# The start of the second MLP's tile pool in SBUF, 64 bytes later

## The chip, the cores and the metric

The kernel runs on one core of one Trainium2 chip. A core has five engines that run side by side and meet at semaphores: TensorE (PE in the profile; its weight loads are listed apart as PEld), VectorE (DVE), ScalarE (ACT), GpSimd (POOL) and SyncE (SP, which here issues transfers alone). Operands lie in SBUF, a memory of 128 partitions; TensorE's sums go to PSUM and are read from there by VectorE and ScalarE. A matmul has a stationary operand (the weights, 128 x 128 here, loaded first) and a moving one (here mostly 128 x 512), whose columns stream past the weights. The metric is the device time of one execution in microseconds (us).

## What is computed

Three parts follow on each other, on an input of 4 sequences of 3072 tokens with 256 features, in float32:

```python
X = np.fft.fft(np.fft.fft(x, axis=1), axis=2).real        # [4, 3072, 256]
h = X.reshape(-1, 256) @ w_in                              # first MLP, d_ff 2048
y = np.maximum(0.01 * h, h) @ w_out
x_prev = concat([0, y[:, :-1]], axis=1)                    # second MLP, on y by sequence
xk, xr = mu_k * y + (1 - mu_k) * x_prev, mu_r * y + (1 - mu_r) * x_prev
k = np.maximum(xk @ w_k, 0)                                # w_k 256 x 1024
v = (k * k) @ w_v                                          # w_v 1024 x 256
out = sigmoid(xr @ w_r) * v                                # w_r 256 x 256
```

## The kernel before

Every large product is made of three TensorE products in the type fp32r: each operand is split into a high part (a rounded copy, made by ScalarE) and a low part (what is left, made by VectorE, line L111), and high x high, low x high and high x low are summed in PSUM. Names ending in `h` and `l` are these parts.

The program is written out in full, in a fixed order. The Fourier transform along the sequence (`f..` sums, L299) is woven between the rounds of the first MLP. A round of the first MLP multiplies one 512-token tile by 128 columns of the hidden layer: three matmuls `ps<-Q` (L560), three `ps<-P` (L548) and twelve `o` matmuls (L571, from the round two before), 18 in all, each with a moving operand of 512 columns. Its result `y` goes to DRAM. Near the end of the first MLP two groups of six matmuls of the second one are already issued (`ps`, L884).

The second MLP then goes over 24 tiles of 512 tokens. For each tile it runs 8 rounds: six matmuls `kps` (L884: the moving operands `mh`, `ml` are the tile's mixed input, the weights `wkh`, `wkl`), ScalarE's `rl` (L888), VectorE's square `k` (L889), the split into `k2h` and `k2l`, and, two rounds later, six matmuls `v` (L926: moving `k2h`, `k2l`, weights `wvh`, `wvl`). Two rounds of each tile also have six gate matmuls `rps` (L934). The mixed input of the next tile (`mt`, `mx`, `mh`, `ml`; L730, L731) is made during the tile before.

Where the operands lie: tiles are placed one behind another in pools. The pool `p2` holds what the second MLP makes (`sig`, `rl`, `k2`, `k2h`, `k2l`, the loaded tiles `xa` and `xb`, `mt`, `mx`, the split inputs `mh` and `ml`, and the output `o`). It begins where the first MLP's pool `wp` began, at byte 43936 of each partition. The weights of the second MLP are in the pool `w2p`, at byte 192480 and up. All these tiles are whole multiples of 512 bytes long, and every slice of weights that one matmul takes begins a multiple of 512 bytes behind its tile's start, so that each operand has one place modulo 512. The tile that tile 0 of the second MLP takes its `mh` and `ml` from lies in another pool, `stage`. The places that the program gives (start address modulo 512 bytes), for fp32r matmuls:

| matmuls | moving operand | weights | in the kernel before |
|---|---|---|---|
| first MLP: `ps` L548, L560 and `o` L571 | 416 | 416 | 3456 matmuls |
| `dps` L592 (weights of 2 columns) | 416 | 32 or 64 | 32 |
| transform L299, batches 1 to 3 | 352 to 456, in steps of 8 | 480 | 216 |
| second MLP, inputs from `stage`: `ps`, and tile 0's `kps` L884; `v<-er` L926 | 128 | 480 | 54 |
| second MLP, inputs from `p2`: `kps` L884 | 416 | 480 | 1104 |
| second MLP: `v` L926 | 416 | 480 | 1146 |
| second MLP: `rps` L934 | 416 | 480 | 288 |

Of the kernel before, what the change touches and what calls it, by code (L numbers as in the profile page):

```python
# [9 lines left out]
F32 = mybir.dt.float32  # L10
# [7 lines left out]
P = 128  # L18
# [60 lines left out]
def fft_mlp_kernel(ctx, tc, xa, xb, x7, x8, x87, tb, tbs, alt, ce, so, mu, w_in, w_out, w_k, w_v, w_r, out):  # L79
# [832 lines left out]

    ps2 = ctx.enter_context(tc.tile_pool(name="ps2", bufs=1, space=PSUM))
    p2 = w2["p2"] = ctx.enter_context(tc.tile_pool(name="p2", bufs=2))

    NB = D // P

# [166 lines left out]
```

## Time and profile before

| | before |
|---|---|
| median of 3 runs | 1526.74 us (1526.39 to 1526.97) |
| the profiled execution's own time | 1527.49 us |
| its span, first to last instruction | 1525.7 us |
| TensorE busy | 1495.8 us, 98% |
| VectorE, ScalarE busy | 1032.4 us (68%), 890.5 us (58%) |
| mean granted TensorE clock | 0.997 of full speed |

The span is the time between the first and the last instruction that the profile shows; the execution's own time has 1.8 us more around it. [...]

### The profile page before, as it was taken

What the parts mean: (1) busy time and instruction counts of PE and PEld (TensorE: products, weight loads), DVE (VectorE), ACT (ScalarE), POOL (GpSimd) and SP (SyncE); (2) the same over time, 40 slices, a digit from 0 to 9 for tenths busy, and PEclk for the clock granted to TensorE, in tenths of its full rate; (3) what the DMA queues carried; (4) which work ended last, traced back from release to release, by engine and by line L of the source; (5) the groups of instructions that cost most, each with busy time, mean ns of one, the idle gap of its engine ahead of it and who ended that gap; (6) DMA issues with size and microseconds to landing.
All of it is one profiled execution on the core that took longest, in us unless ns stands there. A gap on an engine that the chain in (4) does not pass through costs nothing.

```text
span 1525.7 us, 17754 instructions
## 1 busy us (share of the span) xinstructions
PE 1495.8 (98%) x6506; PEld 1212.2 (79%) x6506; DVE 1032.4 (68%) x1426; ACT 890.5 (58%) x1469; POOL 168.1 (11%) x165
## 2 busy tenths in 40 slices
PE   5899999999999999999999999999999999999998
PEld 2677888888888888888888887888888888888887
DVE  8776667676667666666667666666666666666664
ACT  2565566566566656665666656555555555555553
POOL 4333401033001132010000000000000000000000
PEclk9999999999999999999999999999999999999999
DMA  7435614276113565132320103121111212121200
GB/s 249 139 94 115 115 52 153 75 184 99 31 66 122 183 114 89 38 126 86 107 78 0 55 1 124 56 70 65 61 63 62 69 56 69 56 69 56 70 29 28
DMA packets 97810, 128.71 MB, mean 84 GB/s; under 512 B 29190, under 2 KB 64775, under 8 KB 94650
## 3 DMA queue, kind: packets, MB, share of 16 engines
q1 hardware_dynamic: 74618, 87.29, 17.7%
q0 software_dynamic: 23104, 40.29, 11.6%
q8 instruction: 51, 0.84, 0.2%
q14 instruction: 37, 0.30, 0.1%
HBM read 99.67 MB, written 27.88 MB: 84 GB/s over the span
## 4 chain that ended last, share of the span: by engine, by line
PE 95%; DVE 1%; DMA 1%; ACT 0%; issue 0%; POOL 0%; ACTq 0%; DVEq 0%
PE o L571 34%; PE v L926 17%; PE kps L884 17%; PE ps L560 9%; PE ps L548 9%; PE rps L934 4%; PE wps L383 1%; PE dps L592 0%; DMA pm<-in_xa 0%; DMA xl<-in_xb 0%; PE cps L434 0%; PE f0Qe L299 0%; PE f0Pe L299 0%; PE f0Po L299 0%; PE f1Qe L299 0%; PE f2Qe L299 0%
## 5 line engine op out<-in xcount | busy, mean ns | idle before, releaser
L637 DVE SCALAR_TENSOR_TENSOR g<-ev,ps 128x512 f32<-128x512 f32 x192 | 131.7, 686 | 193.3 <-PE ps L560 193.2
L888 ACT ACTIVATE rl<-kps 128x512 f32<-128x512 f32 x190 | 113.8, 599 | 245.2 <-PE kps L884 241.6
L889 DVE SCALAR_TENSOR_TENSOR k<-kps,rl 128x512 f32<-128x512 f32 x190 | 131.4, 692 | 163.3 <-ACT rl L888 161.0
L619 DVE TENSOR_TENSOR gl<-g,gh 128x1024 fp32r<-128x1024 f32 x192 | 239.9, 1249 | 1.4 <-ACT gh L104 1.4
L104 ACT ACTIVATE gh<-g 128x1024 fp32r<-128x1024 f32 x192 | 202.8, 1056 | 51.2 <-PE o L571 50.2
L571 PE MATMUL o<-gh,uoh 128*128 128x512 f32 x768 | 211.3, 389 | 0.0
L571 PE MATMUL o<-gh,uol 128*128 128x512 f32 x768 | 211.1, 389 | 0.0
L571 PE MATMUL o<-gl,uoh 128*128 128x512 f32 x768 | 211.1, 389 | 0.0
L107 ACT ACTIVATE g<-ps 128x512 f32<-128x512 f32 x192 | 114.9, 598 | 163.0 <-DVE g L637 161.6
L571 PEld LDWEIGHTS o<-gh,uoh 128*128 128x128 f32 x768 | 144.1, 188 | 30.4
L571 PEld LDWEIGHTS o<-gh,uol 128*128 128x128 f32 x768 | 144.2, 188 | 30.0
L571 PEld LDWEIGHTS o<-gl,uoh 128*128 128x128 f32 x768 | 144.1, 188 | 29.9
L553 DVE SCALAR_TENSOR_TENSOR ev<-cb,w,ps 128x512 f32<-128x512 f32 x192 | 143.4, 747 | 2.6 <-PE ps L548 0.8
L111 DVE TENSOR_TENSOR k2l<-k,k2h 128x512 fp32r<-128x512 f32 x190 | 129.4, 681 | 0.6 <-ACT k2h L104 0.6
L926 PE MATMUL v<-k2h,wvh 128*128 128x512 f32 x382 | 124.1, 396 | 0.1
L926 PE MATMUL v<-k2h,wvl 128*128 128x512 f32 x382 | 124.0, 395 | 0.0
L926 PE MATMUL v<-k2l,wvh 128*128 128x512 f32 x382 | 124.0, 395 | 0.0
L884 PE MATMUL kps<-mh,wkh 128*128 128x512 f32 x380 | 119.7, 396 | 1.5 <-ACT mh L104 0.8
L884 PE MATMUL kps<-ml,wkh 128*128 128x512 f32 x380 | 119.6, 396 | 0.1
L107 ACT ACTIVATE g<-g 128x512 f32<-128x512 f32 x192 | 119.6, 623 | 0.0
L884 PE MATMUL kps<-mh,wkl 128*128 128x512 f32 x380 | 119.5, 396 | 0.0
L104 ACT ACTIVATE k2h<-k 128x512 fp32r<-128x512 f32 x190 | 118.3, 623 | 0.0
(392 smaller groups left out, 2280.3 us busy)
## 6 DMA issues: line engine op xcount, KB each, us to landing
y<-yo SPq DMA_DIRECT2D x24, 512.0 KB
xa<-y SPq DMA_DIRECT2D x24, 512.0 KB
out_dram<-o SPq DMA_DIRECT2D x23, 512.0 KB
tab_c<-in_tbs POOLq DMA_DIRECT2D x6, 1158.0 KB, 5.6
tab_d<-in_tbs POOLq DMA_DIRECT2D x6, 1158.0 KB, 5.5
tab_a<-in_tbs POOLq DMA_DIRECT2D x6, 1158.0 KB, 6.5
tab_b<-in_tbs POOLq DMA_DIRECT2D x6, 1158.0 KB, 5.4
xl<-in_xa SPq DMA_DIRECT2D x24, 256.0 KB
```

The costliest lines, as they stand in the source:

```text
L104: A.activation(o, i, ACTF.Copy)
L107: A.activation(o, i, ACTF.Prelu, alpha=0.01)
L111: V.tensor_tensor(lo, src, hi.bitcast(F32), op=ALU.subtract)
L548: T.matmul(x["ps"], l[:, f], r, start=(i == 0), stop=(i == 2))
L553: V.scalar_tensor_tensor(x["ev"], x["cb"], w128[:, u:u + 1], x["ps"], op0=ALU.mult, op1=ALU.add)
L560: T.matmul(x["ps"], l[:, f], r, start=False, stop=(i == 2), skip_group_check=True)
L571: T.matmul(po[s][h], w[:, u % HF, h * P:(h + 1) * P], g[:, s], start=(u == 0 and i == 0), stop=(u == NF - 1 and i == 2))
L619: V.tensor_tensor(gl, x["g"], x["gh"].bitcast(F32), op=ALU.subtract)
L637: V.scalar_tensor_tensor(g[:, 1], x["ev"], 2.0, x["ps"], op0=ALU.mult, op1=ALU.subtract)
L884: T.matmul(ps, w[:, k, sl], x[:, k], start=(i == 0), stop=(i == 5))
L889: V.scalar_tensor_tensor(k2, ps, 0.0, r, op0=ALU.max, op1=ALU.mult)
L926: T.matmul(vps[m], w[:, f, m * P:(m + 1) * P], x, start=(f == 0 and i == 0), stop=(f == NK - 1 and i == 2))
```

## The change

One line takes a tile of 16 float32 (64 bytes in each partition) at the start of the pool `p2`. No instruction reads or writes it. Everything else in `p2` begins 64 bytes later (`sig` at byte 44000 where it was 43936, and so on), so that `mh`, `ml`, `k2h` and `k2l` of `p2` are at 480 modulo 512. The weights in `w2p`, the tiles in `stage` and all of the first MLP stay where they are. The instructions of all engines, their order, their sizes and their semaphore waits are the same, one for one.

```diff
@@ -912,6 +912,7 @@
     ps2 = ctx.enter_context(tc.tile_pool(name="ps2", bufs=1, space=PSUM))
     p2 = w2["p2"] = ctx.enter_context(tc.tile_pool(name="p2", bufs=2))
+    p2.tile([P, 16], F32, tag="pad", bufs=1, name="pad3")
 
     NB = D // P
```

## Rows read from the trace of the kernel before

**Rows 1.** The page: busy time, share and instructions; the chain that ended last, by engine

```profile
PE 1495.8 (98%) x6506; PEld 1212.2 (79%) x6506; DVE 1032.4 (68%) x1426; ACT 890.5 (58%) x1469; POOL 168.1 (11%) x165
...
PE 95%; DVE 1%; DMA 1%; ACT 0%; issue 0%; POOL 0%; ACTq 0%; DVEq 0%
```

**Rows 2.** Windows by stage: length, busy us per engine (count), granted clock, DMA

```profile
945.00:1200.00 255.00, 255.00 (x1095) 205.45 (x1094) 171.27 (x250) 147.71 (x245) 0.00 (x0) 1.00 0.20 67
1200.00:1500.00 300.00, 300.00 (x1287) 241.73 (x1286) 198.30 (x287) 172.34 (x286) 0.00 (x0) 1.00 0.17 56
```

**Rows 3.** Timeline of PE, second MLP: start us, us until done, instruction, count

```profile
1199.72 0.63 PE L884 MATMUL kps<-mh,wkh 128*128 128x512 f32 x2
1200.19 0.63 PE L884 MATMUL kps<-mh,wkl 128*128 128x512 f32 x2
...
1219.32 0.63 PE L884 MATMUL kps<-mh,wkh 128*128 128x512 f32 x2
```

**Rows 4.** Timeline of PE, first MLP

```profile
400.75 0.39 PE L560 MATMUL ps<-Qh,wh 128*128 128x512 f32 x1
...
408.91 0.39 PE L560 MATMUL ps<-Qh,wh 128*128 128x512 f32 x1
```

**Rows 5.** Timeline of PE where the second MLP's first matmuls stand among the first's

```profile
906.03 1.07 PE L571 MATMUL o<-gh,uoh 128*128 128x512 f32 x4
...
908.75 0.63 PE L884 MATMUL ps<-mh,wkh 128*128 128x512 f32 x2
...
910.15 1.07 PE L571 MATMUL o<-gh,uoh 128*128 128x512 f32 x4
...
912.87 0.63 PE L884 MATMUL ps<-mh,wkh 128*128 128x512 f32 x2
...
914.27 0.39 PE L571 MATMUL o<-gh,uoh 128*128 128x512 f32 x1
```

**Rows 6.** Groups of instructions from 917 us on: count, busy us, mean ns, idle before

```profile
L926 PE MATMUL v<-k2h,wvh 128*128 128x512 f32 x382 | 124.1, 396 | 0.1
...
L884 PE MATMUL kps<-mh,wkh 128*128 128x512 f32 x380 | 119.7, 396 | 1.5 <-ACT mh L104 0.8 <-ACT yo L104 0.7
...
L934 PE MATMUL rps<-mh,wrh 128*128 128x512 f32 x96 | 30.2, 396 | 0.0
```

**Rows 7.** Waits from 917 us on: engine, line, waited for, total us, times, longest

```profile
ACT rl L888 <- PE kps L884: 241.6, 187, 2.1
DVE k L889 <- ACT rl L888: 161.0, 164, 5.5
```

**Rows 8.** Timeline of PE around the two-column weights, first MLP

```profile
151.94 0.40 PE L592 MATMUL dps<-wh,dcs 128*2 128x512 f32 x1
...
152.41 0.39 PE L560 MATMUL ps<-Qh,wh 128*128 128x512 f32 x1
...
153.80 1.07 PE L571 MATMUL o<-gh,uoh 128*128 128x512 f32 x4
...
156.52 0.39 PE L560 MATMUL ps<-Qh,wh 128*128 128x512 f32 x1
```

**Rows 9.** Timeline of PE, a transform group of 9 matmuls with 384 columns

```profile
234.04 0.52 PE L299 MATMUL f1Po<-tab_c,sh1Po 128*128 128x384 f32 x2
...
235.63 0.40 PE L560 MATMUL ps<-Qh,wh 128*128 128x512 f32 x1
```

**Rows 10.** Timeline of PE, tile 0 of the second MLP

```profile
920.75 0.64 PE L884 MATMUL kps<-mh,wkh 128*128 128x512 f32 x2
...
921.69 0.63 PE L884 MATMUL kps<-ml,wkh 128*128 128x512 f32 x2
```

**Rows 11.** The page, costliest groups: `o` matmuls of the first MLP

```profile
L571 PE MATMUL o<-gh,uoh 128*128 128x512 f32 x768 | 211.3, 389 | 0.0
```

## The prediction

> **What bounds the kernel now.** I read the page's shares and chain first. TensorE is busy for 98% of the span and makes 95% of the chain that ended last [rows 1], so the time is TensorE's, and the question is whether its instructions wait or are slow. [...]
>
> In the second MLP two starts of the same place in a round lie 1219.32 - 1199.72 = 19.60 us apart, with 14 groups of six matmuls between them (6 of `kps`, 6 of `v`, 2 of the gate), 84 in all: 233.3 ns for one [rows 3]. In the first MLP two starts lie 408.91 - 400.75 = 8.16 us apart, two rounds of 18: 226.7 ns [rows 4]. Both are fp32r matmuls of 128 x 128 weights and 512 columns. [...]
>
> Is it the stage, or the matmul? At the end of the first MLP the second's first matmuls stand among the first's, with the same other engines at work. Twelve `o` matmuls from 906.03 to 908.75 take 2.72 us (226.7 ns each), the six of the second MLP that follow take 1.40 (233.3), the next twelve again 2.72, the next six again 1.40 [rows 5]. The pace changes with the matmul, at once and back. The order of PSUM banks doesn't do it either: the first MLP keeps its pace through three matmuls into one bank as through four into four [rows 4, 5], the second through six into one (`kps`) as through two in turn (`v`) [rows 3]. What differs is where the operands lie. By the table of places, the fast ones have both operands at 416 modulo 512, the slow ones 416 with 480, or 128 with 480.
>
> **The change part by part.** It adds no instruction, no wait and no transfer, and moves nothing in any queue. Its one effect is the address of all that lies in `p2`.
>
> TensorE: the matmuls whose moving operand moves are those of the groups `v` (3 x 382 = 1146), `rps` (3 x 96 = 288) and `kps` (3 x 380 = 1140) [rows 6], less the 36 `kps` of tile 0 that read `stage`: 2538. Their pair becomes 480 with 480, equal, as the first MLP's is. The trace has no pair at 480 with 480, so the pace is bounded from rows:
> - below, by the least that a matmul pays over its columns in steady flow: 226.7 ns [rows 4]. Nothing in these stages is faster.
> - above, by the slowest steady stretch: four `kps` of tile 0, at 128 with 480, in 921.69 - 920.75 = 0.94 us, 235.0 ns [rows 10].
> - between them lies what equal places cost when the flow has just been disturbed. Behind two `dps` matmuls, six `ps` at 416 with 416 take 153.80 - 152.41 = 1.39 us, 231.7 ns each, and only then does the pace go to 2.72 us for twelve, 226.7 [rows 8].
>
> I take 226.7. It is the one pace that the trace shows for equal places in undisturbed flow, it holds there for `ps` and `o` matmuls alike, with different tiles on both sides, and the second MLP has the undisturbed flow too (no wait in 555 us [rows 2]). The gain is 2538 x (233.3 - 226.7) = 2538 x 6.67 ns = 16.9 us.
>
> The other engines: the same 64 bytes move the operands of VectorE and ScalarE. I cost that at nothing. ScalarE waits 241.6 us in this part for `kps` itself, and VectorE 161.0 us for ScalarE [rows 7], so both are ahead of TensorE. Twelve matmuls shrink from 2.80 us (12 x 233.3 ns) to 2.72; VectorE's busy share of 171.27 / 255.00 = 67% would become 69%. If an operation of theirs took some per cent longer, it would come out of those waits.
>
> The sum: 1527.49 us of the profiled execution (span 1525.7 and 1.8 around it) less 16.9 is 1510.6. The median of the runs is 0.75 us below the profiled one, so I forecast 1526.74 - 16.9 = **1509.8 us**.
>
> [...]
>
> **The rivals.**
> *The weights' own place decides (no change).* Every slow row with 128-column weights has the weights at 480, and the pace is 233.3 both with the moving operand at 416 [rows 3] and at 128 [rows 5]. If weights that begin at 480 are slow by themselves, moving the other operand does nothing: 1526.7 us. For it: two quite different distances give one pace, which is odd if the distance matters. Against it: the two `dps` matmuls have their weights at 32, only two columns of them, and still take 235 ns (152.41 - 151.94 = 0.47 us for two) [rows 8]. [...]
>
> *Equal places, but the flow stays unsettled (small gain).* The 231.7 ns of rows 8 were at equal places. If the second MLP kept that, the gain would be 2538 x 1.6 = 4.1 us: 1522.6 us.
>
> *The new pair is a worse one (slower).* Both operands at 480 begin at the same offset, and if a clash depends on absolute place, 480 with 480 could do worse than 416 with 480. At the 235.0 ns of rows 10 it costs 2538 x 1.67 = 4.2 us: 1530.9 us. It decides once the pace is above 234.5 ns (3.05 us over 2538 matmuls is 1.2 ns each). For it: the trace never shows 480 with 480. Against it: nothing in these stages holds a pace above 235.
>
> **How the numbers follow.** The full gain has a chance of 0.62, a part of it 0.10, no change 0.19 (the weights' own place and the two ports together), slower 0.09. A measurement can tell about 0.2%, 3.05 us, from no change; faster by more than that needs a pace under 232.1 ns. That gives 0.72 faster, 0.19 the same, 0.09 slower. The likeliest case by itself spans 1508.5 to 1511.5 us. To leave no more than 2 in 10 out, the range has to take in the partial gain and no change: up to 1527.5. Below, 1507 leaves 1 ns a matmul for a pace a little under 226.7.
>
> **What would show it.** In the timeline of the second MLP, a round of twelve would go from 2.80 to 2.72 us and the groups `v`, `kps`, `rps` from a mean of 396 ns [rows 6] to the 389 of `o` [rows 11], with the `ps` and tile 0's `kps`, whose places don't change, still at 1.40 us for six or a little more. The first MLP would end at the same time as before. If rounds stay at 2.80, the pair's equality is not the reason for the two paces and the weights' own place is next to try. If TensorE shows new waits for `k2h` or `mh`, ScalarE or VectorE were less far ahead than I read. The prediction is wrong if the pace at 480 with 480 isn't that at 416 with 416.

## The result and the profile after

The changed kernel takes 1510.5 us (median of four runs, 1510.43 to 1511.04) beside 1526.74 for the kernel before (median of the three runs shown above). A fourth run of the kernel before took 4021.5 us, for a reason that isn't known, and is left out. The ratio of the runs is 0.9895 with a 95% interval of 0.9875 to 0.9914: faster by about 1.05%. Forecast were 1509.8 us.

The page's busy line, which answers to [rows 1], has the same counts; TensorE is busy for 16.5 us less, the others are as they were:

```profile
PE 1479.3 (98%) x6506; PEld 1212.3 (80%) x6506; DVE 1032.8 (68%) x1426; ACT 890.5 (59%) x1469; POOL 168.2 (11%) x165
```

Windows of the changed kernel, cut where the second MLP begins (columns as in [rows 2]), and below them the two of its steady flow:

```profile
0.00:917.30 917.30, 892.85 (x3926) 728.45 (x3926) 636.49 (x852) 545.06 (x897) 168.22 (x165) 0.99 0.37 99
917.30:1509.30 592.00, 586.48 (x2581) 483.89 (x2580) 396.31 (x574) 345.46 (x573) 0.00 (x0) 1.00 0.19 65
...
945.00:1200.00 255.00, 255.00 (x1127) 211.15 (x1126) 176.09 (x257) 152.49 (x252) 0.00 (x0) 1.00 0.21 69
1200.00:1500.00 300.00, 300.00 (x1325) 248.43 (x1324) 202.11 (x294) 174.33 (x290) 0.00 (x0) 1.00 0.17 57
```

The same cut in the kernel before, with windows that end at 917.00 and 1525.70 us, has TensorE busy for 892.59 and 603.24 us. So the first MLP is unchanged within 0.3 us and the whole gain lies in the second: 603.24 - 586.48 = 16.8 us. TensorE still never waits in the steady windows; it fits 1127 matmuls into 255 us where there were 1095.

The timeline of the second MLP, answering to [rows 3]: twelve matmuls now take 2.72 us, six rounds from 1203.36 to 1219.68 take 16.32 us for 72, 226.7 ns each.

```profile
1203.36 0.61 PE L884 MATMUL kps<-mh,wkh 128*128 128x512 f32 x2
...
1206.08 0.61 PE L884 MATMUL kps<-mh,wkh 128*128 128x512 f32 x2
...
1219.68 0.61 PE L884 MATMUL kps<-mh,wkh 128*128 128x512 f32 x2
```

The groups, answering to [rows 6], and the waits, answering to [rows 7]: the matmuls' mean duration, which is longer than the distance to the next start (226.7 ns), goes from 396 to 389 or 390 ns, VectorE's and ScalarE's durations stay (`k` 692 and 693 ns, `rl` 599 in both), and what TensorE gained is taken out of the time for which they wait.

```profile
L927 PE MATMUL v<-k2h,wvh 128*128 128x512 f32 x382 | 121.7, 389 | 0.1
...
L884 PE MATMUL kps<-mh,wkh 128*128 128x512 f32 x380 | 117.3, 390 | 1.5 <-ACT mh L104 0.8 <-ACT yo L104 0.7
...
L935 PE MATMUL rps<-mh,wrh 128*128 128x512 f32 x96 | 29.6, 389 | 0.0
```

```profile
ACT rl L888 <- PE kps L884: 227.0, 187, 2.1
DVE k L889 <- ACT rl L888: 147.7, 163, 5.5
```

Two places are not at the new pace. The six `ps` among the first MLP's matmuls, whose places did not change, still take 910.38 - 908.98 = 1.40 us, as in [rows 5]. And in tile 0 the 48 matmuls from 924.13 to 935.26 take 11.13 us, 231.9 ns each. Of these, 18 are tile 0's own `kps`, whose inputs lie in `stage`, at 128 with 480: six of them take 1.40 us, as before (924.13 to 925.53). The other 30 (`v` and `rps`) are at 480 with 480 but stand in between, in groups of six or twelve, and take up to 1.39 us for six (925.53 to 926.92). From tile 1's first `kps` on, all matmuls are at 480 with 480; behind a wait of 0.82 us and twelve matmuls the flow goes at 2.72 us for twelve:

```profile
908.98 0.63 PE L884 MATMUL ps<-mh,wkh 128*128 128x512 f32 x2
...
910.38 1.07 PE L571 MATMUL o<-gh,uoh 128*128 128x512 f32 x4
...
924.13 0.63 PE L884 MATMUL kps<-mh,wkh 128*128 128x512 f32 x2
...
925.53 0.63 PE L927 MATMUL v<-k2h,wvh 128*128 128x512 f32 x2
...
926.92 0.63 PE L884 MATMUL kps<-mh,wkh 128*128 128x512 f32 x2
...
935.26 0.63 PE L884 MATMUL kps<-mh,wkh 128*128 128x512 f32 x2
...
939.03 0.73 PE L884 MATMUL kps<-mh,wkh 128*128 128x512 f32 x2 [0.82 <-ACT mh L104]
...
942.24 0.62 PE L884 MATMUL kps<-mh,wkh 128*128 128x512 f32 x2
...
944.96 0.62 PE L884 MATMUL kps<-mh,wkh 128*128 128x512 f32 x2
```

### The profile page after: what moved, and what is told of

It reads as the page before. It is cut to its first block, busy times and chain, and to the rows that moved or that the text cites. A ratio compares the mean times of both kernels' runs of the same rounds, so it can differ in the third digit from the quotient of the medians.

```text
span 1509.3 us, 17754 instructions
## 1 busy us (share of the span) xinstructions
PE 1479.3 (98%) x6506; PEld 1212.3 (80%) x6506; DVE 1032.8 (68%) x1426; ACT 890.5 (59%) x1469; POOL 168.2 (11%) x165
## 4 chain that ended last, share of the span: by engine, by line
PE 95%; DVE 1%; DMA 1%; ACT 0%; issue 0%; POOL 0%; ACTq 0%; DVEq 0%
PE o L571 34%; PE v L927 17%; PE kps L884 17%; PE ps L560 9%; PE ps L548 9%; PE rps L935 4%; PE wps L383 1%; PE dps L592 0%; DMA pm<-in_xa 0%; DMA xl<-in_xb 0%; PE cps L434 0%; PE f0Qe L299 0%; PE f0Pe L299 0%; PE f1Qe L299 0%; PE f2Qe L299 0%; DMA y<-yo 0%
## 5 line engine op out<-in xcount | busy, mean ns | idle before, releaser
L888 ACT ACTIVATE rl<-kps 128x512 f32<-128x512 f32 x190 | 113.9, 599 | 230.4 <-PE kps L884 227.0
L889 DVE SCALAR_TENSOR_TENSOR k<-kps,rl 128x512 f32<-128x512 f32 x190 | 131.6, 693 | 148.4 <-ACT rl L888 147.7
```

The lines of the kernel that those rows point to most:

```text
L889: V.scalar_tensor_tensor(k2, ps, 0.0, r, op0=ALU.max, op1=ALU.mult)
```

## The experiments

The change moved several things by 64 bytes at once: the moving operands, and all that VectorE and ScalarE touch in `p2`. The theory is that the distance between the places of moving operand and weights decides. The questions were whether it is that pair, which modulus counts, whether the absolute place matters, and which of the weights a matmul must match: its own or the next one's.

**The weights moved in place of the pool.** The pad goes behind the weights on the other side of SBUF, so that they lie 64 bytes lower, at 416; `p2` is as before.

```diff
+        w2p.tile([P, 16], F32, name="wpad")
...
-    p2.tile([P, 16], F32, tag="pad", bufs=1, name="pad3")
```

> The kernel before, with the second MLP's weights 64 bytes lower (416 modulo 512) and the pool p2 where it was (416). Theory of the pair (the distance between the places of the moving operand and of the weights decides): twelve matmuls of the second MLP take 2.72 us, the time is 1510 to 1511 us. Rival, the place of p2's tiles (of the moving operand alone, or of what VectorE and ScalarE read and write there): they lie as before, so 2.80 us for twelve and 1526.7 us.

Measured: 1510.97 us, ratio to the kernel before 0.9896 (0.988 to 0.9913). Six rounds of its second MLP take 1219.57 - 1203.25 = 16.32 us, as in the changed kernel:

```profile
1203.25 0.62 PE L885 MATMUL kps<-mh,wkh 128*128 128x512 f32 x2
...
1219.57 0.62 PE L885 MATMUL kps<-mh,wkh 128*128 128x512 f32 x2
```

The rival falls: nothing in `p2` moved here, and the gain is all there.

**Every distance, one to a tile.** `mh`, `ml`, `k2h` and `k2l` are taken 512 bytes longer and used from an offset that differs by tile (`O` below, in float32, tile by tile). In a second kernel the weights are moved to 256 and the distances run the other way.

```diff
+    O = [0, 0, 8, 16, 24, 32, 40, 48, 56, 64, 72, 80, 88, 96, 104, 112, 120, 2, 4, 6, 10, 126, 124, 122]
...
-        hi = p2.tile([P, W], F32R, tag="k2h", bufs=3, name="k2h")
+        hi = p2.tile([P, W + 128], F32R, tag="k2h", bufs=3, name="k2h")[:, o:o + W]
...
```

> Weights at 480; the moving operands of each of the 24 tiles lie at their own distance from that: tile 1 at 0, then 32, 64 and so on to 480 for tile 16, then 8, 16, 24, 40, 504, 496, 488 for tiles 17 to 23. Theory of the pair, modulo 512: 2.72 us for twelve at distance 0 alone and about 2.80 at the others. Rival, a smaller modulus (256, 128): 2.72 also at 256, or at 128, 256 and 384. Rival, a narrow clash at the old distance (448) and a few others: most distances at 2.72. Over all tiles the first gives about 1526 us, the last about 1512.

> The sweep with the weights at 256 and the distances in falling order, 480 at tile 1 to 0 at tile 16, then 136, 264, 272, 400, 12, 4 and 0. If the distance alone decides, every distance has the pace of the first sweep within 1 ns, whatever the absolute place and what ran before: about 227 to 228 at 0 and 256, 229.4 at 64 and 320, 233 to 234 at the other multiples of 32. If absolute places or history matter, the fast ones are other ones.

Measured: 1524.87 and 1524.62 us, one run each. The paces are worked out from the trace as the mean of the distances from one matmul's start to the next, over the matmuls whose moving operand has that distance from its weights (108 in most cases; gaps over 300 ns, which are waits, left out). The column for 0 has tile 0's unsettled matmuls in it, and 160 of the first and 384 of the second those from `stage`:

```
distance      0     32    64    96    128   160   192   224
first       228.1 233.3 229.4 233.5 233.0 234.1 233.2 233.2   ns a matmul
second      228.2 233.3 229.3 233.4 232.7 234.1 233.1 233.2
distance    256    288   320   352    384   416   448   480
first       227.6 233.3 229.4 233.5 233.0 234.1 233.2 233.0
second      227.8 233.3 229.3 233.4 232.7 234.1 233.1 233.2
distance      4     8     12    16    24    40   264   272   504
first        -    232.9   -   231.4 234.2 233.8   -     -   234.7
second     236.8   -    229.8   -     -     -   233.0 231.5   -
distance    136   400   488   496
first        -     -   233.3 232.9
second     233.9 233.1   -     -
```

The two kernels agree within 0.5 ns at each distance that both have, though the weights lie elsewhere and the neighbours in time are others: the distance decides. And the table repeats itself after 256 bytes: 256 is as fast as 0, 320 as 64, 264 and 272 are as 8 and 16. It does not repeat after 128: 128 is at 233.0.

How the flow goes over from one distance to the next shows in the first sweep's timeline. Tile 8 is at 224, tile 9 at 256, tile 10 at 288. The round from 1142.11 has six `kps` of tile 9 and still six `v` of tile 8, and takes 2.79 us. The next is all at 256: its first six take 1146.28 - 1144.90 = 1.38 us, its second six 1.36, and the round behind it 2.72, the settled pace. A round at 288 takes 2.80. The means at 0 and 256 hold such unsettled matmuls too, which is why they are a little above 226.7:

```profile
1142.11 0.63 PE L885 MATMUL kps<-mh,wkh 128*128 128x512 f32 x2
...
1144.90 0.63 PE L885 MATMUL kps<-mh,wkh 128*128 128x512 f32 x2
...
1146.28 0.62 PE L928 MATMUL v<-k2h,wvh 128*128 128x512 f32 x2
...
1147.64 0.62 PE L885 MATMUL kps<-mh,wkh 128*128 128x512 f32 x2
...
1150.36 0.62 PE L885 MATMUL kps<-mh,wkh 128*128 128x512 f32 x2
...
1172.34 0.63 PE L885 MATMUL kps<-mh,wkh 128*128 128x512 f32 x2
...
1175.14 0.63 PE L885 MATMUL kps<-mh,wkh 128*128 128x512 f32 x2
```

**256 bytes apart for the whole run.**

```diff
-    p2.tile([P, 16], F32, tag="pad", bufs=1, name="pad3")
+    p2.tile([P, 80], F32, tag="pad", bufs=1, name="pad3")
```

> The pad of the changed kernel is 320 bytes in place of 64: moving operands at 224, weights at 480, 256 bytes apart. The sweep had this distance at 227.6 ns in its tile's stretch, beside 228.1 at 0. If the places matter modulo 256: 2.72 us for twelve, 1510 to 1511.5 us. If only modulo 512, and the sweep's tile was favoured by what went before it: 2.80 and about 1526.7 us.

Measured: 1510.71 us, ratio 0.9891 (0.9876 to 0.9905), and six rounds in 1220.00 - 1203.68 = 16.32 us:

```profile
1203.68 0.62 PE L884 MATMUL kps<-mh,wkh 128*128 128x512 f32 x2
...
1220.00 0.62 PE L884 MATMUL kps<-mh,wkh 128*128 128x512 f32 x2
```

The places need to agree modulo 256 bytes, not 512 as the theory had it.

**The worst distance for the whole run.** The offsets of the sweep, 4 bytes for every tile (`O = [1] * 24`).

> The changed kernel with the moving operands of p2 4 bytes further (484 with the weights at 480), the slowest distance that a sweep showed (236.8 ns a matmul, one tile long). If the sweeps' paces hold for a whole run: 1510.5 + 2538 x 10.0 ns = 1536 us, slower than the kernel before. If that tile was unsettled by its neighbours: nearer to 233 ns, 1527 us. ScalarE and VectorE write at the 4 bytes too, but lie ahead of TensorE.

Measured: 1535.77 us, slower than the kernel before by a ratio of 1.0055 (1.0038 to 1.0072). Twelve matmuls take 1206.47 - 1203.63 = 2.84 us, 236.7 ns each:

```profile
1203.63 0.63 PE L885 MATMUL kps<-mh,wkh 128*128 128x512 f32 x2
...
1206.47 0.63 PE L885 MATMUL kps<-mh,wkh 128*128 128x512 f32 x2
```

The sweep's pace holds over the run, and it gives the time within 0.3 us.

**The first MLP put apart.** Half of the weights of the `o` matmuls move by 32 bytes, the changed kernel's second MLP stays.

```diff
-    wo.tile([P, 80], F32, name="pad2")
+    wo.tile([P, 72], F32, name="pad2")
```

> The changed kernel, but in the first MLP the weights of the hidden layer's second half (o matmuls, 1152 of 2304) lie 32 bytes lower than before, at 384 while the moving operands are at 416: distance 32. If the rule is one of the matmul and not of the second MLP, those o matmuls take 2.80 us for twelve and the time is 1510.5 + 1152 x 6.6 = 1518 us, up to 1522 if the ps matmuls between them are unsettled. If the first MLP doesn't follow the rule: 1510.5 us.

Measured: 1517.88 us, ratio to the kernel before 0.9938 (0.9921 to 0.9954), 7.4 us above the changed kernel's 1510.5. Its timeline has both kinds of round next to each other: twelve `o` at equal places take 330.95 - 328.23 = 2.72 us, twelve with the moved weights 335.11 - 332.32 = 2.79:

```profile
328.23 1.07 PE L571 MATMUL o<-gh,uoh 128*128 128x512 f32 x4
...
330.95 0.39 PE L560 MATMUL ps<-Qh,wh 128*128 128x512 f32 x1
...
332.08 0.40 PE L548 MATMUL ps<-Ph,wl 128*128 128x512 f32 x1
332.32 1.09 PE L571 MATMUL o<-gh,uoh 128*128 128x512 f32 x4
...
335.11 0.39 PE L560 MATMUL ps<-Qh,wh 128*128 128x512 f32 x1
```

The rule is the matmul's, not the stage's.

**All of the second MLP at one place.** Weights and moving operands at 128, where `stage` is.

```diff
+        w2p.tile([P, 88], F32, name="wpad")
...
-    p2.tile([P, 16], F32, tag="pad", bufs=1, name="pad3")
+    p2.tile([P, 56], F32, tag="pad", bufs=1, name="pad3")
```

> Moving operands in p2 and weights both at 128 modulo 512, where the pool stage is already, so that the second MLP's first 54 matmuls are equal too. Theory of the pair: 2.72 us for twelve at a third place (after 416 and 480), and the first tile of the second MLP, which in the changed kernel runs at 232 to 233 ns a matmul, goes at 226.7 too: up to 60 matmuls times 6.7 ns and some 90 unsettled ones times 5 ns less than the changed kernel, 0.4 to 0.9 us: 1509.6 to 1510.1 us. Rival, the absolute place matters as well: a pace other than 226.7 ns and a time between 1511 and 1531 us.

Measured: 1510.73 us, ratio 0.9895 (0.988 to 0.991). A third absolute place gives the same pace in steady flow (2.72 us for twelve, 1203.50 to 1206.22), but the further gain doesn't show: the runs take 1510.67 to 1511.18 us, beside 1510.43 to 1511.04 of the changed kernel. Tile 0, whose `kps` are equal now too, does go faster (924.42 to 927.15, 2.73 us for twelve, where the changed kernel has 2.79 from 924.13 to 926.92), but where the first MLP's matmuls (416 with 416) and these (128 with 128) follow on each other, both kinds are above the settled pace: six `ps` take 910.65 - 909.26 = 1.39 us, and the twelve `o` behind them 913.41 - 910.65 = 2.76, where the changed kernel has 2.72.

```profile
909.26 0.63 PE L885 MATMUL ps<-mh,wkh 128*128 128x512 f32 x2
...
910.65 1.08 PE L571 MATMUL o<-gh,uoh 128*128 128x512 f32 x4
...
913.41 0.63 PE L885 MATMUL ps<-mh,wkh 128*128 128x512 f32 x2
...
924.42 0.62 PE L885 MATMUL kps<-mh,wkh 128*128 128x512 f32 x2
...
927.15 0.62 PE L885 MATMUL kps<-mh,wkh 128*128 128x512 f32 x2
```

**Own weights or the next ones.** The `kps` matmuls alternate between the halves k = 0 and k = 1 of their operands. In four kernels the second half's weights lie 64 or 128 bytes further, and the moving operand's halves follow them (own weights equal) or are swapped about (the next weights equal). The edit shown is that of own weights equal at 64 bytes; the others differ in the offsets and in the length of the tiles.

```diff
-                w2[nm + x] = w2p.tile([P, k, f], F32R, name=f"w{nm}{x}")
+                if nm == "k":
+                    t = w2p.tile([P, 2 * FK + 128], F32R, name=f"w{nm}{x}")
+                    w2[nm + x] = t[:, :2 * (FK + 16)].rearrange("p (k f) -> p k f", k=2)[:, :, :FK]
...
-                hi = w2["p2"].tile([P, 2, W], F32R, tag=nm + "h", name="mh")
...
+                    hi, lo = (w2["p2"].tile([P, 1152], F32R, tag=nm + x, name="m" + x)[:, 0:1056].rearrange("p (k w) -> p k w", k=2)[:, :, :W] for x in "hl")
```

> The changed kernel, but of the two halves of the kps operands the second lies 64 bytes further, in the moving operand and in the weights alike: each kps matmul has its own weights at its own place, and the next matmul's weights 64 bytes away. If what clashes is a running matmul and the load of the weights of the next one, kps goes back to 1.40 us for six while v stays at 1.36 or is disturbed behind it: 1510.5 plus up to 1104 x 6.7 ns = 7.4 us, more if v is unsettled too. If a matmul and its own weights are the pair that matters: 1.36 for six and 1510.5 us.

> As the run in which own weights were equal, but the halves of the moving operand are swapped about: each kps matmul lies 64 bytes from its own weights, one way or the other, and at the same place as the next matmul's weights (but at the ends of a group of six). If a running matmul and the next matmul's load are the pair: six kps in 1.36 to 1.38 us and a time of 1510.5 to 1513 us. If a matmul and its own weights are: at the paces of distance 448 and 64 of the sweep, 233.2 and 229.4 ns, 1104 matmuls at 231.3, with v unsettled up to 232: 1515 to 1523 us.

> As the run in which own weights were equal, with the second halves 128 bytes further in place of 64: each kps matmul at its own weights' place, the next matmul's weights always at distance 128 modulo 256 (233.0 ns in the sweep where all pairs have it). If a running matmul and the next load are the pair: kps at 233 ns and v disturbed behind it, 1517 to 1525 us. If own weights are: 226.7 ns, 1510.5 us. If the running matmul must match both, or if a step from one moving operand's place to the next by itself unsettles the flow: slow, like the first.

> As the run in which the next weights were equal, with 128 bytes in place of 64: each kps matmul at distance 128 modulo 256 from its own weights and at the place of the next matmul's. If a running matmul and the next load are the pair: kps mostly at 226.7 ns, 1510.5 to 1514 us. If own weights are: 233 ns and 1517 to 1525 us. If both must match, or a step between moving operands unsettles: 1517 to 1525 us too, so that this run with the one before it tells the pair apart only where one of the two is fast.

Measured, one run each, with the mean distance of starts of the `kps` and the `v` matmuls (from the trace, as above):

```
                  us      kps ns   v ns
own equal, 64   1523.24    232.4   230.7
next equal, 64  1521.36    232.1   230.0
own equal, 128  1518.79    231.1   229.2
next equal, 128 1514.27    230.0   226.8
```

None of the four keeps `kps` at 226.7. So it isn't enough that a matmul matches its own weights, nor that it matches the next ones; both single-pair theories fall as they were stated. `v`, equal in all four, is unsettled in three, and only with the next weights equal at 128 does it stay at 1.36 us for six, beside 1.38 of `kps`:

```profile
1207.39 0.63 PE L890 MATMUL kps<-mh,wkh 128*128 128x512 f32 x2
...
1208.77 0.62 PE L933 MATMUL v<-k2h,wvh 128*128 128x512 f32 x2
...
1210.13 0.63 PE L890 MATMUL kps<-mh,wkh 128*128 128x512 f32 x2
```

Whether both matches are needed, or a step from one operand's place to the next one's unsettles the flow by itself, these runs don't tell. Two other places in the traces point different ways. In the run with the first MLP put apart, the last `ps` of a round matches its own weights but not the next ones, 32 bytes off, and its successor starts 235 ns behind it (332.08 to 332.32) where the five before it take some 227. In [rows 5] the last of twelve `o` is followed by weights 64 bytes off, and the twelve still take 2.72 us.

## Why the prediction was right

**What bounds the kernel**: right. TensorE without a wait set the time before and after (busy for all of the 255 and 300 us of the steady windows, in [rows 2] and in the changed kernel), and what changed was the distance of its starts, from 233.3 to 226.7 ns.

**The price**: right in its size. 2538 matmuls by 6.67 ns, 16.9 us, were forecast, and TensorE is busy for 16.8 us less in the second MLP. The whole execution gained a little less: 16.5 us in the profiled one (1527.49 to 1511.04), whose first MLP took 0.3 us longer, and 16.2 between the medians, 0.7 short of the forecast. Tile 0 accounts for about 0.1 of that: its 30 equal matmuls from 924.13 to 935.26, which stand between unequal ones, take 6.93 us in place of 30 x 226.7 ns = 6.80. The rest is no more than the spread of one kernel's runs (0.6 us). The rival of the unsettled flow thus held for some dozens of matmuls of tile 0 and was wrong for the rest.

The range, 1507 to 1527.5 us, took in no change as well, so a time within it says little by itself. What bears out that the distance of the two places decides is the pace of the rounds, 2.72 us for twelve, and the runs that moved one operand at a time.

**The pace taken for 480 with 480**: right, and for the reason given, the two places' distance; 416, 480 and 128 with themselves have all been measured at 226.7 ns since. The rival that the weights' own place decides falls with the change itself, for the weights stayed at 480, and again with the sweeps. What I had held for it, that 128 with 480 and 416 with 480 go at one pace, is answered by the table: distances 160 and 448 are 234.1 and 233.2 ns, two of many that happen to be alike.

**The slower rival** fell: no worse pair at 480. The price that I gave it was too low for what a bad place can cost; 4 bytes make 236.7 ns and 1535.77 us.

**The other engines**: right. Their durations are unchanged (busy for 1032.4 and 1032.8 us, 890.5 in both), their waits for TensorE shrank from 241.6 to 227.0 and from 161.0 to 147.7 us, and no wait of TensorE's came up (for `kps` 0.8 and 0.7 us, as before).

**The reading of the modulus** was not tested by the forecast, and places that agree modulo 512 are more than is needed: 256 is enough.

**The two ports**, which share the 0.19 of no change with the weights' own place, are shown by no run. What the runs show is that both operands' places count: moving the weights alone by 64 bytes took the kernel from 1527.21 to 1510.97 us, moving `p2` alone from 1526.74 to 1510.5. Why the distance sets the pace was not shown.

## What to carry to other kernels

When TensorE never waits and the same kind of matmul starts at two paces in two stages, compare where the operands lie before anything else: a pad that no instruction touches was worth 1% (1526.74 to 1510.5 us). For fp32r matmuls of 128 x 512 let moving operand and weights begin at the same place modulo 256 bytes (226.7 ns settled at distances 0 and 256, 229.3 to 236.8 at the others), in all matmuls that follow on each other, and check it with the distance of starts, since busy shares don't show it (TensorE is at 98% before and after). A tile put ahead of a pool can undo it, as 32 bytes less in `pad2` did for half of the `o` matmuls (2.79 us for twelve in place of 2.72), and 4 bytes off cost more than any other distance tried (236.8 ns). Other types and other sizes were not tried.

## What the runs showed of the hardware that was not expected

- The period is 256 bytes (in steady flow 0 and 256 both take 2.72 us for twelve; 64 and 320 are both at 229.4 ns in the first sweep), and inside it there are more paces than two: 226.7 ns settled at 0, 229.4 at 64, 231.4 at 16, 229.8 at 12, 232.7 to 234.1 at the other multiples of 32, 236.8 at 4.
- Equal places do not always give the pace at once. Behind unequal ones, six equal matmuls took 1.38 us in the sweep (1144.90 to 1146.28) and only the next six 1.36; where unequal groups keep coming between, as in tile 0 of the changed kernel, the equal ones stay above the settled pace (30 in 6.93 us, 231.0 ns each). Yet in [rows 5] twelve `o` right behind unequal `ps` take 2.72 us.
- Two groups that are each equal in themselves, at 416 and at 128, disturb each other where they meet: 2.76 us for twelve `o` in place of 2.72, shown in one kernel.
